# Weights read two bytes late, the first gates as a second product, and a planner that lets TensorE wait

## The chip, the cores and the metric

The kernel runs on one core of a Trainium2 chip (trn2). The metric is the device time of one execution in microseconds (us); lower is better.

## What is computed

```python
def _attn_ref(q, k, v, s):                  # 4 batches, 8 heads, 576 tokens, 64 wide
    scores = scale * np.matmul(q, k.transpose(0, 1, 3, 2))
    cum = np.cumsum(np.maximum(s, 0.0), axis=-1)
    bias = -(cum[:, :, :, None] - cum[:, :, None, :])
    scores = np.where(causal, -1000000000.0, scores + np.minimum(bias, 0.0))
    ...                                     # softmax over keys
    return np.matmul(attn, v)
def _moe_ref(x, w_gate, w_val, w_out, rms_g):   # 2304 tokens, 512 -> 1536 -> 512
    xn = x / np.sqrt(np.mean(x * x, axis=-1, keepdims=True) + 1e-06) * rms_g
    g = xn @ w_gate
    return g * (1.0 / (1.0 + np.exp(-g))) * (xn @ w_val) @ w_out
```

`reference` puts the heads of a token side by side, sends the result through `_moe_ref` and that result through a second block of the same kind without the normalisation (`_moe2_ref`, its own weights). The weights arrive as 8-byte floats; q, k, v and s as 4-byte floats.

## The kernel before

**Stages.** The 576 queries of a batch are cut in a group A (the first 256) and a group B (the other 320). The kernel starts with the A groups of batches 0 and 1: 16 "early" heads (`EarlyUnit`) with plain fp32 products. Then come group B of batches 0 and 1 and both groups of batches 2 and 3 (`Unit`), with split operands. Between them, on TensorE, run the gate and value products of the first MoE block (`moe1`) for each group of tokens whose heads are done and normalised (`normalise`). What `moe1` makes goes to DRAM (`h_d`), and after the attention is through, the out product of block 1 (`out_mm`) and block 2 follow.

**Split weights.** Every MoE product is exact enough only with more than one pass: a matrix is kept as H, its value rounded to TensorE's fp32r, and L, the rest, and one product is xH·H + xL·H + xH·L. `convert` makes H and L from the 8-byte words, 128 x 512 words at a time: a load into a tile `raw` (L382, 512 KB); ACT turns the top 16 bits into an fp16 (L384) and moves 16 bits of the lower half (L386), both into a tile `cvy`; DVE shifts and masks the upper words in `raw` (L389) and joins them with `cvy` by and/or (L392); a copy on ACT or POOL rounds to H (L396, L397); a subtraction gives L (L400). `load_gv` does this for the 12 slices f of gate and value weights of a block, two blocks each. For the first MoE block the raw words of slice f lie in the places of H and L of slice f+2 (`raw_places`).

**Order of the work.** Nothing is issued where it is written. Each call of `op` records one operation with a price per engine, what it reads and writes, and a priority. `Plan.run` then plays the program: per engine a heap `waiting` (by the time at which the inputs are there) and a heap `ready` (by priority); of what is ready on an engine, the lowest priority number goes first, and the order found is the order in which each engine's instructions are issued. `LAT` has the latencies between engines. Early head u has the priority P_ATT + u, the loads 1000 less, the MoE products of the first block P_MOE + f, which is higher than any head's: they fill in.

**The bias of the early heads.** `setup` (from L430) loads s, makes its running sum on DVE in `cum` (L473 to L481, the scan at L476), stores it (L484), and on POOL builds the identity (the affine select of `masks.py`), clears rows 64 and up of the early q and k tiles `lq` and sets row 64 of the q side to one (`clear_rows`, L458 and L459; its output is called "lower rows"). Row 64 of the k side gets the head's running sum by a DMA of 1 KB (L705), which waits for both. So one product over 128 rows (L716) gives scores and key bias at once. `self.least` takes minimum and mask on DVE, `exponent` is an ACT pass (L612), `values` transposes on TensorE (L726), copies to `pTA` (L732), multiplies with v (L736).

**Normalisation.** `normalise` squares x on ACT, sums squares by a product with `half` (L767), runs some 18 tiny steps on DVE (L795 to L829), transposes (L833), copies, spreads the factors by a product with `sel` (L840), scales x on DVE (L844) and splits it into xH (ACT, L847) and xL (L849). Then `gate_value` (L860) can read it, and `hidden` (L867 to L872) does tanh and the two multiplications.

## Time and profile before

| | |
|---|---|
| median of 3 runs (1147.38 to 1148.27) | 1148.12 us |
| the profiled execution / its span | 1150.81 us / 1148.8 us |
| granted TensorE clock, mean | 0.994 |
| busy: TensorE, its weight loads, DVE, ACT, POOL | 1119.8, 1002.3, 608.5, 545.9, 188.8 us |
| chain of waits: TensorE, DMA, DVE, ACT | 89%, 3%, 3%, 2% |
| moved by DMA | 112.54 MB, 98 GB/s on average |

The time of the profiled execution is the device time of that one run; the span is what the profile covers of it, from the first instruction to the last. Busy is time in which an engine works on an instruction. The chain of waits is followed back from the last instruction, at each step to what released it.

### The profile page before, as it was taken

What the parts mean: (1) busy time and instruction counts of PE and PEld (TensorE: products, weight loads), DVE (VectorE), ACT (ScalarE), POOL (GpSimd) and SP (SyncE); (2) the same over time, 40 slices, a digit from 0 to 9 for tenths busy, and PEclk for the clock granted to TensorE, in tenths of its full rate; (3) what the DMA queues carried; (4) which work ended last, traced back from release to release, by engine and by line L of the source; (5) the groups of instructions that cost most, each with busy time, mean ns of one, the idle gap of its engine ahead of it and who ended that gap; (6) DMA issues with size and microseconds to landing.
All of it is one profiled execution on the core that took longest, in us unless ns stands there. A gap on an engine that the chain in (4) does not pass through costs nothing.

```text
span 1148.8 us, 18822 instructions
## 1 busy us (share of the span) xinstructions
PE 1119.8 (97%) x6708; PEld 1002.3 (87%) x6708; DVE 608.5 (53%) x1670; ACT 545.9 (48%) x1203; POOL 188.8 (16%) x280
## 2 busy tenths in 40 slices
PE   5899999999999999999999999999999999999998
PEld 3589999999999999999877788888888888888898
DVE  5798899988735965542586424432222222222222
ACT  5787989888534844431687435432111211211121
POOL 3243445344202400000011000001000100000000
PEclk9899999999999999999999999999999999999999
DMA  5774455434221234438656634211000100100010
GB/s 156 229 239 130 141 146 155 123 102 128 75 74 46 71 102 116 113 109 273 224 165 201 203 110 130 74 37 49 26 1 1 64 1 1 46 1 1 1 37 20
DMA packets 70221, 112.54 MB, mean 98 GB/s; under 512 B 11696, under 2 KB 39344, under 8 KB 70128
## 3 DMA queue, kind: packets, MB, share of 16 engines
q1 hardware_dynamic: 70128, 111.35, 31.6%
q8 instruction: 53, 0.87, 0.3%
q14 instruction: 40, 0.33, 0.1%
HBM read 87.63 MB, written 23.67 MB: 97 GB/s over the span
## 4 chain that ended last, share of the span: by engine, by line
PE 89%; DMA 3%; DVE 3%; ACT 2%; issue 1%; SPq 1%; POOL 0%; DVEq 0%; ACTq 0%
PE mo L860 51%; PE sps L1013 8%; PE tp L1013 8%; PE mo L1013 5%; PE sps L575 4%; PE tp L639 4%; PE tp L655 4%; DMA cvs<-in_w_gv 1%; PE mo L767 1%; PE tp L736 1%; PE sps L716 1%; DMA raw<-in_w_gv 1%; ACT cvy L384 1%; DMA lq<-cum 1%; ACT cvy L386 1%
## 5 line engine op out<-in xcount | busy, mean ns | idle before, releaser
L860 PE MATMUL mo<-xH,L 128*128 128x320 f32 (+1 forms) x768 | 229.4, 299 | 0.0
L860 PE MATMUL mo<-xH,H 128*128 128x320 f32 (+1 forms) x768 | 229.0, 298 | 0.1
L860 PE MATMUL mo<-xL,H 128*128 128x320 f32 (+1 forms) x768 | 228.3, 298 | 0.5 <-POOL xL L849 0.5
L869 DVE SCALAR_TENSOR_TENSOR t<-t,mo 128x256 f32<-128x256 f32 (+2 forms) x156 | 81.3, 521 | 257.6 <-ACT t L867 257.1
L867 ACT ACTIVATE t<-mo 128x256 f32<-128x256 f32 (+2 forms) x156 | 72.3, 464 | 276.8 <-PE mo L860 271.9
L860 PE MATMUL mo<-x1H,L 128*128 128x512 f32 (+1 forms) x480 | 176.6, 368 | 0.0
L860 PE MATMUL mo<-x1H,H 128*128 128x512 f32 (+1 forms) x480 | 176.6, 368 | 0.0
L860 PE MATMUL mo<-x1L,H 128*128 128x512 f32 (+1 forms) x480 | 176.6, 368 | 0.0
L1002 ACT ACTIVATE hH<-hh 128x512 fp32r<-128x512 f32 (+1 forms) x120 | 69.6, 584 | 165.1 <-DVE hh L872 132.2
L860 PEld LDWEIGHTS mo<-xL,H 128*128 128x128 f32 x768 | 145.1, 189 | 1.4 <-POOL xL L849 0.7
L860 PEld LDWEIGHTS mo<-xH,H 128*128 128x128 f32 x768 | 145.0, 189 | 1.1 <-issue 0.3
L860 PEld LDWEIGHTS mo<-xH,L 128*128 128x128 f32 x768 | 145.0, 189 | 0.5
L872 DVE TENSOR_TENSOR hh<-t,mo 128x256 f32<-128x256 f32 (+2 forms) x156 | 81.3, 521 | 100.2 <-PE mo L860 99.2
L1004 DVE TENSOR_TENSOR hL<-hh,hH 128x512 fp32r<-128x512 f32 (+1 forms) x120 | 79.7, 667 | 87.7 <-ACT hH L1002 87.2
L860 PEld LDWEIGHTS mo<-x1H,L 128*128 128x128 f32 x480 | 90.5, 189 | 14.9
L860 PEld LDWEIGHTS mo<-x1H,H 128*128 128x128 f32 x480 | 90.5, 189 | 14.8
L860 PEld LDWEIGHTS mo<-x1L,H 128*128 128x128 f32 x480 | 90.5, 189 | 14.8
L612 ACT ACTIVATE sc<-sc,col 128x512 f32<-128x512 f32 (+4 forms) x160 | 95.6, 598 | 14.1 <-DVE col L601 13.2
L1045 POOL TENSOR_TENSOR x1L<-x1l,x1H 128x512 fp32r<-128x512 f32 (+1 forms) x20 | 25.8, 1302 | 390.6 <-ACT x1H L1043 302.4
L1013 PE MATMUL sps<-hH,oH 128*128 128x512 f32 (+1 forms) x192 | 67.8, 365 | 2.1 <-ACT hH L1002 2.1
L1013 PE MATMUL sps<-hL,oH 128*128 128x512 f32 (+1 forms) x192 | 69.5, 363 | 0.0
L1013 PE MATMUL tp<-hH,oL 128*128 128x512 f32 (+1 forms) x192 | 69.4, 363 | 0.0
(127 smaller groups left out, 2096.1 us busy)
## 6 DMA issues: line engine op xcount, KB each, us to landing
raw<-in_w_gv SPq DMA_DIRECT2D x40, 512.0 KB, 4.8
cvs<-in_w_o SPq DMA_DIRECT2D x24, 512.0 KB, 3.8
hh<-h_d SPq DMA_DIRECT2D x48, 256.0 KB, 3.1
cb<-cum_d SPq DMA_DIRECT2D x32, 288.0 KB, 3.4
lq<-in_qk SPq DMA_DIRECT2D x32, 288.0 KB, 3.2
h_d<-hh SPq DMA_DIRECT2D x72, 128.0 KB, 2.2
vl<-in_vp SPq DMA_DIRECT2D x32, 160.0 KB, 3.0
cvs<-in_w_gv SPq DMA_DIRECT2D x8, 512.0 KB, 4.2
```

Source lines behind the costliest of these rows:

```text
L575: op(PE, c_mm(n), lambda en, pt=pt, o=o, c=c, n=n, z=z, kk=kk: en.matmul(pt()[:, :n], qst[j]()[:, o:o + 128], kk()[:, c:c + n], start=z == ...
L612: op(ACT, c_act(o + m, 2) + 35, lambda en: en.activation(sc()[:m, :o + m], sc()[:m, :o + m], ACTF.Exp, scale=-1.0, bias=col()[:m, 0, t:t + 1],
L639: op(PE, C_TR, lambda en, pt=pt, a=a, m=m, kb=kb, t=t: en.transpose(pt()[:, a:a + P], self.sc[t]()[:, kb * P:kb * P + P], ident()), r=[sel ...
L655: op(PE, c_mm(n), lambda en, w=w, z=z, kb=kb, d0=d0, n=n, o=o, kn=kn: en.matmul(po()[:, o:o + n], vst[j]()[:kn, kb, :], pT[g][z]()[:kn, d0 ...
L860: op(PE, c_mm(n), lambda en, a=a, x=x, c=c, k=k, i=i: en.matmul(ps()[:, :n], a()[:, c], x()[:, k, :n], start=(k == 0 and i == 0), stop=(k ...
L867: op(ACT, c_act(n), lambda en: en.activation(t()[:, :n], gp()[:, :n], ACTF.Tanh, scale=0.5), r=[gp], w=[t], pri=pri)
L869: op(DVE, c_tt(n), lambda en: en.scalar_tensor_tensor(out=t()[:, :n], in0=t()[:, :n], scalar=1.0, in1=gp()[:, :n], op0=ALU.add, op1=ALU.mu ...
L872: op(DVE, c_tt(n), lambda en: en.tensor_tensor(out=hh()[:, :n], in0=t()[:, :n], in1=vp_()[:, :n], op=ALU.mult), r=[vp_, t], w=[hh], pri=pri)
L1002: op(ACT, c_act(n) + 35, lambda en: en.activation(H()[:, :n], hh()[:, :n], ACTF.Copy), r=[hh], w=[H], pri=pri)
L1004: op(DVE, c_tt(n), lambda en: en.tensor_tensor(out=L()[:, :n], in0=hh()[:, :n], in1=f32(H()[:, :n]), op=ALU.subtract), r=[hh, H], w=[L], p ...
L1013: op(PE, c_mm(n), lambda en, d=d, c=c, w=w, x=x, i=i: en.matmul(acc_[d]()[:, :n], Wo[w]()[:, c], HL[x]()[:, :n], start=(f == 0 and i == 0) ...
L1045: op(POOL, c_ptt(n), lambda en, k=k, x=x: en.tensor_tensor(out=L()[:, k, :n], in0=x()[:, :n], in1=f32(H()[:, k, :n]), op=ALU.subtract), r= ...
```

## The change

**Weights.** The load reads the same words from two bytes on (2047 of 2048 16-bit units per partition), so that what was in bytes 2 to 5 of each word is now a whole 32-bit unit. One ACT pass still puts the fp16 of the top bits in the upper half of `cvy`, whose lower half is zeroed once (`clear`). One DVE instruction shifts the 32-bit unit right by 13 and ors `cvy` in, and writes the result into the raw tile. The ACT pass of L386 and the DVE pass of L389 are gone; H and L read the raw tile, which is therefore held until L is done. `cvy` is two tiles of their own for the first weights, one for all later ones.

**First gates.** The running sum is made twice: for the first 256 tokens into `cumA`, and later for all. The first four early heads get no row of the sum; a second product (L761 of the changed kernel) of a column of the identity, broadcast, with `cumA` adds it to their scores. The other twelve load the row from `cumA`.

**Planner.** An operation of TensorE whose last input came from another engine enters the `ready` heap 1500 ns (`SLACK`) later than its inputs are there; until then it is in `at_once`, from which it is taken only where `ready` holds nothing. The raw loads have other priorities, conversions too, and the sums of squares another price.

```diff
+    SLACK = 1500.0
...
         def offer(n):
             for k, (e, _) in enumerate(ops[n][0]):
-                heapq.heappush(waiting[e], (ready_on[n][k], k, n))
+                slack = 0.0
+                if e == PE and released[n] not in (PE, NONE):
+                    heapq.heappush(at_once, (ready_on[n][k], k, n))
+                    slack = self.SLACK
+                heapq.heappush(waiting[e], (ready_on[n][k] + slack, k, n))
...
+                if e == PE and not ready[e]:
...
+                    if at_once and (not waiting[e] or at_once[0][0] < waiting[e][0][0]):
+                        t, k, n = at_once[0]
+                        if t <= free[e]:
+                            heapq.heappop(at_once)
+                            heapq.heappush(ready[e], (ops[n][3] + 1.0e6 * k, n))
...
+                    if ready_on[u][k] > before:
+                        released[u] = e
...
+FIRST = 4
...
-        op(SP, 8 * P * n, lambda en: en.dma_start(out=stage(), in_=src.bitcast(I32)),
+        op(SP, 8 * P * n, lambda en: en.dma_start(
+            out=stage().bitcast(U16)[:, :4 * n - 1], in_=src.bitcast(U16)[:, 1:]),
            w=[stage], pri=pri if early is None else early)
         op(ACT, c_act(n) + 165, lambda en: en.activation(
-            part(y, F16, 2, 1), part(stage, BF16, 4, 3), ACTF.Copy), r=[stage], w=[y], pri=pri)
-        op(ACT, c_act(n) + 165, lambda en: en.activation(
-            part(y, U16, 2, 0), part(stage, U16, 4, 1), ACTF.Copy, scale=2.0 ** -13,
-            bias=-4095.5 * 2.0 ** -13), r=[stage], w=[y], pri=pri)
-        op(DVE, c_ts(n), lambda en: en.tensor_scalar(
-            out=hi(), in0=hi(), scalar1=3, scalar2=MIDDLE,
-            op0=ALU.logical_shift_left, op1=ALU.bitwise_and), r=[stage], w=[stage], pri=pri, port=True)
+            part(y, F16, 2, 1), part(stage, BF16, 4, 2), ACTF.Copy), r=[stage], w=[y], pri=pri)
         op(DVE, c_tt(n), lambda en: en.scalar_tensor_tensor(
-            out=i32(y), in0=i32(y), scalar=-(1 << 27) + 7, in1=hi(),
-            op0=ALU.bitwise_and, op1=ALU.bitwise_or), r=[stage, y], w=[y], pri=pri, port=True)
+            out=whole(U32), in0=whole(U32), scalar=13, in1=y().bitcast(U32),
+            op0=ALU.logical_shift_right, op1=ALU.bitwise_or), r=[stage, y], w=[stage],
+           pri=pri, port=True)
...
+        def clear_cum(en):
+            en.memset(cumA()[NB * NH:64], 0.0)
+            en.memset(cumA()[64:], 0.0)
+        op(POOL, 500, clear_cum, w=[(cumA, 1)], pri=-2e6)
...
+        cumulate(cumA, 2 * P, -1e6)
+        cumulate(cum, S, -900)
...
-            op(SP, 1024, lambda en: en.dma_start(
-                out=ql()[D:D + 1, 1, 288 * i:288 * i + 256], in_=cum()[n:n + 1, 0:256]),
-               r=[cum, "lower rows"], w=self.parts[2:], pri=pri)
+            if not self.first:
+                op(SP, 1024, lambda en: en.dma_start(
+                    out=ql()[D:D + 1, 1, 288 * i:288 * i + 256], in_=cumA()[n:n + 1]),
+                   r=[cumA, "lower rows"], w=self.parts[2:], pri=pri)
...
-                    start=True, stop=True), r=[*self.parts, "lower rows"], w=[pt], pri=pri)
+                    start=True, stop=not self.first), r=[*self.parts, "lower rows"], w=[pt],
+                   pri=pri)
+                if self.first:
+                    i = self.b * NH + self.h
+                    op(PE, 0.422 * 4 * kl, lambda en, pt=pt, kl=kl: en.matmul(
+                        pt()[:, :kl], ident()[:, i:i + 1].to_broadcast([P, P]), cumA()[:, :kl],
+                        start=False, stop=True), r=[ident, cumA], w=[pt], pri=pri)
...
-            op(PE, 108 * nt, sums, r=[q, half], w=[ps], pri=pri)
+            op(PE, 206 * nt, sums, r=[q, half], w=[ps], pri=pri)
...
-        W1.append(load_gv(w_gv, f, places, tmps1, P_ATT + 10 + 0.5 * f,
-                          P_ATT - 1000 + 6 + 1.5 * f))
+        W1.append(load_gv(w_gv, f, places, tmps1, P_ATT + 8 + 0.5 * f,
+                          P_ATT - 1000 + 8 + 1.0 * f))
```

The order on three stretches follows; a row is a line of the kernel, the operation, out<-in by tile names and the shape, and a number behind a tile's name tells its uses apart.

TensorE, its first rows, before; `sps` is a bank for scores, `tp` one for transposes, `sc` a tile of scores:

```order
L716 MATMUL sps_165<-lq_101 128x128
L716 MATMUL sps_168<-lq_101 128x256
L716 MATMUL sps_177<-lq_106 128x128
L726 MATMUL tp_181<-ident,sc_170 128x128
L716 MATMUL sps_185<-lq_106 128x256
L726 MATMUL tp_181<-ident,sc_179 128x128 x2
L716 MATMUL sps_201<-lq_101 128x128
```

TensorE, its first rows in the change:

```order
L755 MATMUL sps_151<-lq_116 128x128
L755 MATMUL sps_164<-lq_116 128x256
L761 MATMUL sps_164<-cumA,ident 128x256
L761 MATMUL sps_151<-cumA,ident 128x128
L755 MATMUL sps_180<-lq_121 128x128
L761 MATMUL sps_180<-cumA,ident 128x128
L755 MATMUL sps_186<-lq_121 128x256
L761 MATMUL sps_186<-cumA,ident 128x256
L771 MATMUL tp_193<-ident,sc_171 128x128
```

Each of the first scores is now followed by a product with `cumA`, and both products of the second head come ahead of the first transposes.

ACT, its first rows, before; `tot` takes the row sums, `col` the row's decay:

```order
L384 ACT_TABLE_LOAD
L384 ACTIVATE cvy<-raw_154 128x512
L386 ACTIVATE cvy<-raw_154 128x512
L612 ACTIVATE sc_170,tot_89<-sc_170,col_171 128x128
L612 ACTIVATE sc_179,tot_89<-sc_179,col_171 128x256
L396 ACTIVATE H_190<-cvy 128x512
L612 ACTIVATE sc_187,tot_89<-sc_187,col_188 128x128
L384 ACTIVATE cvy<-raw_161 128x512
L612 ACTIVATE sc_195,tot_89<-sc_195,col_188 128x256
```

ACT, its first rows in the change:

```order
L649 ACT_TABLE_LOAD
L649 ACTIVATE sc_171,tot_89<-sc_171,col_172 128x128
L649 ACTIVATE sc_177,tot_89<-sc_177,col_172 128x256
L649 ACTIVATE sc_188,tot_89<-sc_188,col_189 128x128
L408 ACTIVATE cvy<-raw_166 128x512
L649 ACTIVATE sc_196,tot_89<-sc_196,col_189 128x256
L649 ACTIVATE sc_210,tot_89<-sc_210,col_211 128x128
L415 ACTIVATE H_222<-raw_166 128x512
```

The first pass over the weights moved from the first place on ACT to behind three passes of the softmax, and of the two conversion passes per `raw` tile one is left.

TensorE, around the transposes (L833) of the first normalisation of a B group, before; `xH`, `xL`, `L`, `H` belong to gate and value products, `qst`, `kHH`, `kLL` to scores of later heads:

```order
L833 MATMUL mo_2642<-ident,sq_87 128x128 x3
L639 MATMUL tp_2635<-ident,sc_2519 128x128
L639 MATMUL tp_2635<-ident,sc_2527 128x128
L860 MATMUL mo_2605<-xH_1288,L_1080 128x256
L860 MATMUL mo_2605<-xH_1288,H_1057 128x256
L860 MATMUL mo_2605<-xL_1267,H_1057 128x256
L860 MATMUL mo_2605<-xH_1288,L_1080 128x256
L639 MATMUL tp_2671<-ident,sc_115 128x128
L639 MATMUL tp_2671<-ident,sc_2519 128x128
```

TensorE, around the last gate or value product (L905) of the two early groups in the change; the next such product stands 48 rows later, behind the normalisation of the first B group:

```order
L612 MATMUL sps_2443<-kHH_848,qst_97 128x288
L612 MATMUL sps_2443<-kLL_879,qst_97 128x288
L905 MATMUL mo_2389<-xH_1351,L_1222 128x256
L612 MATMUL sps_2451<-kHH_848,qst_97 128x288
L612 MATMUL sps_2451<-kLL_879,qst_97 128x288
L676 MATMUL tp_2456<-ident,sc_111 128x128
L676 MATMUL tp_2456<-ident,sc_2227 128x128
L676 MATMUL tp_2456<-ident,sc_2236 128x128
L676 MATMUL tp_2456<-ident,sc_111 128x128
L676 MATMUL tp_2456<-ident,sc_2227 128x128
L612 MATMUL sps_2466<-kHH_984,qst_99 128x384
L612 MATMUL sps_2466<-kLL_1025,qst_99 128x384
```

Before, gate and value products of the early groups still stood behind the transposes of that normalisation; in the change they are used up ahead of it.

## Rows read from the trace of the kernel before

**Rows 1.** Page, part 1: busy us (share of the span) and instructions of TensorE.
```profile
PE 1119.8 (97%) x6708; PEld 1002.3 (87%) x6708; DVE 608.5 (53%) x1670; ACT 545.9 (48%) x1203; POOL 188.8 (16%) x280
```

**Rows 2.** Windows: busy us (x instructions) of PE, PEld, DVE, ACT, POOL; PEclk, DMA share, GB/s.
```profile
0.00:12.00 12.00, 0.41 (x2) 0.45 (x3) 4.66 (x15) 0.81 (x1) 6.41 (x21) 1.00 0.48 134
12.00:42.00 30.00, 26.23 (x137) 17.80 (x136) 22.15 (x81) 26.01 (x73) 8.19 (x9) 1.00 0.69 199
42.00:56.00 14.00, 11.74 (x43) 7.54 (x42) 11.27 (x42) 11.22 (x29) 3.80 (x5) 0.63 0.83 245
56.00:80.00 24.00, 21.28 (x156) 18.98 (x156) 21.66 (x52) 21.04 (x49) 10.80 (x13) 1.00 0.73 214
80.00:300.00 220.00, 218.04 (x1655) 210.53 (x1654) 196.46 (x735) 185.60 (x468) 100.39 (x164) 1.00 0.45 134
...
560.00:650.00 90.00, 87.24 (x378) 69.96 (x377) 63.17 (x100) 67.63 (x117) 11.78 (x8) 1.00 0.56 180
...
1144.00:1148.80 4.80, 0.93 (x8) 0.72 (x7) 1.19 (x3) 0.38 (x1) 0.00 (x0) 0.94 0.33 111
```

**Rows 3.** Waits of PE, whole run: waiting line, what ended it, us in total, times, longest.
```profile
PE sps L716 <- DMA lq<-cum: 13.4, 2, 11.6
```

**Rows 4.** Timeline, first 20 us, all engines: start us, us, engine line operation.
```profile
3.80 0.51 POOL L458 MEMSET lq<- 1x256 f32 x1
4.09 1.35 DVE L476 TENSOR_TENSOR_SCAN cum<-cum 32x576 f32<-32x576 f32 x1
...
5.74 0.39 POOL masks.py:199 TENSOR_SCALAR_AFFINE_SELECT ident<-ident 128x128 f32<-128x128 f32 x1
...
7.60 2.49 SPq L705 DMA_DIRECT2D lq<-cum  x4
...
11.59 2.08 PE L716 MATMUL sps<-lq 128*128 128x128 f32 x6 [11.59 <-DMA lq<-cum]
```

**Rows 5.** Timeline, PE alone, 14 to 29 us: the early score products.
```profile
14.61 1.06 PE L716 MATMUL sps<-lq 128*128 128x256 f32 x2
...
19.02 0.82 PE L716 MATMUL sps<-lq 128*128 128x128 f32 x4
...
28.07 0.60 PE L716 MATMUL sps<-lq 128*128 128x256 f32 x2
```

**Rows 6.** Tile raw, whole run: forms with min/median/max ns, and landing times of its loads.
```profile
L386 ACT ACTIVATE cvy<-raw x40: 751/774/802, 13.1 to 615.6; 128x512 uint16<-128x512 uint16 x40
L389 DVE TENSOR_SCALAR raw<-raw x40: 414/423/1196, 13.3 to 616.4; 128x512 int32<-128x512 int32 x40
L392 DVE SCALAR_TENSOR_TENSOR cvy<-cvy,raw x40: 678/693/1595, 14.0 to 616.9; 128x512 int32<-128x512 int32 x40
...
DMA to landing us min/median/max: 3.7/4.8/7.0
```

**Rows 7.** Timeline, PE, 38 to 49 us: the stalls of heads 11 and 12.
```profile
41.25 0.89 PE L716 MATMUL sps<-lq 128*128 128x128 f32 x4 [1.82 <-DMA lq<-cum]
...
48.62 0.33 PE L726 MATMUL tp<-ident,sc 128*128 128x128 f32 x1 [1.50 <-ACT sc L612]
```

**Rows 8.** Timeline, PE, 159 to 185 us: normalisation of the first B group.
```profile
159.96 0.83 PE L767 MATMUL mo<-half,sq 128*128 128x2 f32 x6
...
182.92 0.49 PE L833 MATMUL mo<-ident,sq 128*128 128x128 f32 x3
...
184.11 0.41 PE L840 MATMUL mo<-xL,sel 128*128 128x320 f32 x1
```

**Rows 9.** Groups of instructions on DVE, 100 to 300 us: count, busy us, mean ns, idle before.
```profile
L647 DVE TENSOR_TENSOR pTB<-tp,pTB 128x512 fp32r<-128x512 f32 (+1 forms) x74 | 42.0, 571 | 5.7 <-ACT pTB L644 4.9
L601 DVE CUSTOM_DVE_ANT_0 sc<-sps,cb 128x384 f32<-128x384 f32 (+3 forms) x85 | 37.3, 448 | 2.6 <-PE sps L575 1.8 <-PE tp L639 0.2
...
L813 DVE SCALAR_TENSOR_TENSOR rc<-rc 128x3 f32<-128x3 f32 (+1 forms) x9 | 1.5, 166 | 0.1
```

**Rows 10.** Timeline, ACT, 185 to 186 us: the first normalised copy.
```profile
185.78 0.47 ACT L847 ACTIVATE xH<-x 128x320 fp32r<-128x320 f32 x1 [0.24 <-DVE x L844]
```

More of the change, by code (lines that the diff above doesn't have):

```diff
@@ L397, in convert @@
-            POOL: lambda en: en.tensor_scalar(out=H()[:, cut], in0=y(), scalar1=1.0, scalar2=1.0,
-                                              op0=ALU.mult, op1=ALU.mult)},
-           r=[y], w=[(H, c)], pri=pri)
+            ACT: lambda en: en.activation(H()[:, cut], whole(), ACTF.Copy),
+            POOL: lambda en: en.tensor_scalar(out=H()[:, cut], in0=whole(), scalar1=1.0,
+                                              scalar2=1.0, op0=ALU.mult, op1=ALU.mult)},
+           r=[stage], w=[(H, c)], pri=pri)
@@ L400, in convert, with clear @@
         op(sub, 0, lambda en: en.tensor_tensor(
-            out=L()[:, cut], in0=y(), in1=f32(H()[:, cut]), op=ALU.subtract),
-           r=[y, (H, c)], w=[(L, c)], pri=pri, port=True)
+            out=L()[:, cut], in0=whole(), in1=f32(H()[:, cut]), op=ALU.subtract),
+           r=[stage, (H, c)], w=[(L, c)], pri=pri, port=True)
+    def clear(tiles, pri):
+        for b in tiles:
+            op([(POOL, 500), (DVE, 320)], 0, lambda en, b=b: en.memset(b(), 0.0), w=[b], pri=pri)
     def raw_places(last):
@@ L472, in setup, with cumulate, steps @@
         op([(POOL, 1500), (DVE, 1500)], 0, clear_scores, w=sc4, pri=-1e5)
-        op(DVE, 400, lambda en: en.tensor_scalar(
-            out=cum(), in0=cum(), scalar1=0.0, scalar2=None, op0=ALU.max),
-           r=[cum], w=[cum], pri=-1e6)
-        op(DVE, 670, lambda en: en.tensor_tensor_scan(
-            cum2(), cum(), cum(), 0.0, op0=ALU.add, op1=ALU.max),
-           r=[cum], w=[cum2], pri=-1e6)
-        op(DVE, 400, lambda en: en.tensor_scalar(
-            out=cum(), in0=cum2(), scalar1=cum2()[:, S // 2:S // 2 + 1], scalar2=1.0 / SCALE,
-            op0=ALU.subtract, op1=ALU.mult), r=[cum2], w=[cum], pri=-1e6)
+        def cumulate(out, n, pri):
+            rows = NB * NH
+            def steps(en):
+                en.tensor_scalar(out=cum()[:, :n], in0=cum()[:, :n], scalar1=0.0, scalar2=None,
+                                 op0=ALU.max)
+                en.tensor_tensor_scan(cum2()[:, :n], cum()[:, :n], cum()[:, :n], 0.0,
+                                      op0=ALU.add, op1=ALU.max)
+                en.tensor_scalar(out=out()[:rows, :n], in0=cum2()[:, :n],
+                                 scalar1=cum2()[:, n // 2:n // 2 + 1],
+                                 scalar2=1.0 / SCALE, op0=ALU.subtract, op1=ALU.mult)
+            op(DVE, 400 + 3.6 * n, steps, r=[cum], w=[cum, cum2, (out, 0)] if out is not cum
+               else [cum, cum2], pri=pri)
+        cumulate(cumA, 2 * P, -1e6)
+        cumulate(cum, S, -900)
         op(SP, 4 * NB * NH * S, lambda en: en.dma_start(out=cum_d, in_=cum()),
-           r=[cum], w=["cum_d"], pri=-1e6)
+           r=[cum], w=["cum_d"], pri=-990)
     def lq_parts(b, half):
@@ L687, in __init__ @@
             self.parts = lq_parts(early_q[i % 2], i // 2 % 2)
+            self.first = i < FIRST
             self.vl = early_v[i % 2], i // 2 % 2
@@ L900, in tile_kernel @@
     places = raw_places([buf("at", f"pTB{i}", [P, 1024], I32, f"cvs{i}") for i in range(2)])
+    tops1 = [buf("at", f"cvt{i}", [P, 512], F32, "cvy") for i in range(2)]
     cvt = [0]
@@ L904, in tmps1 @@
         cvt[0] += 1
[L905 removed]
+        return tops1[cvt[0] % 2]
+    clear(tops1, P_ATT + 2)
     heads, units = [], []
```

25 lines of the change are left out of this document (13 added, 12 removed).

## The prediction

> **What bounds the kernel now.** I read five views: the page's busy shares, a table of windows, TensorE's waits, the timeline of the first 50 us, and the stretch around one normalisation.
>
> The page has TensorE busy for 1119.8 us of a span of 1148.8 [rows 1]; only its 29.0 idle us, and work added to it or taken from it, can move the time. The windows say where they are [rows 2]: 11.59 of the first 12 us, 3.77 in 12 to 42, 2.26 in 42 to 56, 2.72 in 56 to 80, 1.96 in 80 to 300, 2.76 in 560 to 650, 3.87 at the end, hardly any elsewhere. The reader is also to see two other things in those rows: the granted clock is 0.63 in 42 to 56, where DMA is at its busiest (245 GB/s, share 0.83), and ACT is busy for 26.01 of the 30 us from 12 to 42, so that there ACT nearly bounds too.
>
> The waits name the first hole: 13.4 us for the DMA that puts the running sum into `lq`, 11.6 of them once [rows 3]. The timeline has the steps [rows 4]: POOL clears the last rows at 4.31, the scan ends at 5.44, the identity is there at 6.13, the four small DMAs are issued from 7.60, and the first score product starts at 11.59.
>
> **The start: −6.** The first products no longer need the running sum, only q, k and the cleared rows. Two more memsets stand ahead of the clearing; at 0.3 to 0.5 each as for the rows of that line [rows 4] the first product starts at about 5.2, and its gate product when the identity is there, 6.13 + 0.6 to 0.8, near 7. The sum of 256 columns takes less than half the scan's 1.35 and is no longer last. TensorE gains 11.59 − 5.5 = 6 us. Bounds: 8 (if nothing but the clearing holds it) and 3 (if the gate products hold up the two score banks, so that only two heads' products gain).
>
> **Eight gate products: +3.2.** A head's score products, 128 and 256 columns, take 0.82 [rows 5], and a gate product has the same columns and type: 4 × 0.82 = 3.3, less a little for overlap. The rows give bounds: 128x256 twice took 1.06 at 14.61 and 0.60 at 28.07 [rows 5], though the clock column says 1.00 for both [rows 2]. If all the eight are at the early pace it is 4.6, if at the later one 2.6. The Trainium skill ("TensorE: Matmul & The Clock Gate", part 1) says that the engine's default is throttled and that activity releases it; by that the early pace holds at the start and the term is 4.6. I stay with 3.2, since the 0.82 are of the same stretch.
>
> **The conversions: −3.5.** An ACT pass of 0.774 and a DVE pass of 0.423 fall away per block [rows 6]. The first weights have 24 blocks, all before about 110 us: 24 × 0.774 = 18.6 us of ACT and 24 × 0.423 = 10.2 of DVE, the other 48 blocks lie later. TensorE had 3.77 + 2.26 + 2.72 = 8.75 us idle from 12 to 80 [rows 2]; 1.82 ended with the running sum's DMA [rows 7], and 0.7 I put down to other transfers. Of the remaining 6.2, which end mostly with ACT or DVE (such as 1.50 for a softmax pass [rows 7]), I take a good half, 3.5. Bounds: 0 (the load, not the pass, is what conversion waits for) and 6.2. The remaining DVE instruction reads and writes every other word, as the old one read one of its inputs; I keep its 0.693 [rows 6].
>
> **The shifted load: 0.** It moves two bytes less per partition. No row of before has such a load; a raw load lands after 3.7 to 7.0, median 4.8 [rows 6]. The near row is the unshifted one, so I take no difference; the far end, landings beyond 7 us, is the second rival. The Trainium skill ("DMA: Bandwidth & Descriptors", "How a descriptor splits into AXI transactions") has it that a read starts at the 256-byte line below its address: bytes 2 to 4095 touch the same sixteen lines as 0 to 4095, so by it nothing changes either way if each partition's read is one descriptor.
>
> **The stretch at half clock: 0.** 14 us at 0.63 [rows 2] are worth about 14 × 0.63 = 8.8 of full clock: some 5 us more could be had back or lost again. Whether it recurs hangs on holes in TensorE's work around 40 to 56; load and softmax stay what they were, so I take it as it is. Bounds −4.5 and +4.5.
>
> **The late stalls: −2.5.** At 560 to 650 and 80 to 300 TensorE idles 2.76 + 1.96 = 4.7 us [rows 2]. With the new rule a product that another engine has just released stands behind others that are ready, which puts 1.5 us of work between; and ACT and DVE have fewer passes there (48 blocks × 0.774 and 0.423, [rows 6]). I take half. Bounds 0 and −4.7.
>
> **The order around the first B group: +5.** This is what the order rows show against the change. Before, gate products of the early groups still stood behind the transposes (L833) of the normalisation of the first B group; now they are used up 32 rows ahead of it, and 47 rows pass without one. Before, the chain from the last sum of squares to the transposes took from 160 to 182.92 [rows 8], and nobody felt it. Now what TensorE has between the squares and the transposes is about 9 us by the rows of order: two heads' value products, 16 gate products, transposes and scores. DVE has in the same piece the 18 tiny steps at about 0.17 to 0.2 (3.4), 11 copies and subtractions and 11 minimum passes at 0.45 to 0.57 [rows 9], two groups' tanh products: some 12 us. So about 3.5 are open. From the transposes to the first xH it took 182.92 to 186.25 [rows 8, 10], 3.3, against some 2 of scores and transposes: 1.5 more. Sum 5. Bounds 0 (the heap at priority lets DVE do the steps first) and 9 (a second B group does the same).
>
> **The sum.** −6 + 3.2 − 3.5 + 0 + 0 − 2.5 + 5 = −3.8, on the profiled execution's 1150.81 about 1147.0. The median of before is 1148.12, 2.7 lower; on its scale that is 1144.3, and I say **1144.0**. A measurement of this kernel tells about 0.2%, 2.3 us, from no change: faster is below 1145.8, slower above 1150.4.
>
> **The rivals.**
>
> 1. *Better: the run-out is covered and the half-clock stretch is gone.* For it: ACT loses a pass of 0.774 per block in just the stretch where it is fullest. Then +5 falls away and 4.5 come on top: 1134.5. Against it: DMA is as busy as before there. Chance 0.22.
>
> 2. *Slower: shifted words land late.* If a load that starts at an odd pair of bytes takes half again its 4.8 us, 24 loads of 512 KB (12.6 MB, at 245 GB/s 51 us of the first 80) no longer fit beside the heads' own, and gate products wait. By 24 × 0.5 us, 12 more: about 1155. It decides from landings above some 7 us [rows 6]. No row excludes it. Chance 0.08.
>
> 3. *Slower: the run-out is wholly exposed.* If the 23 us from squares to transposes [rows 8] remain, the 9 us of other products leave 14 open instead of 3.5: 1144 + 9 to 10, near 1153.5. It decides once that chain is longer than some 18 us. Against it: it was so long because nothing hurried it: 18 steps of 0.17 are 3 us of work [rows 9]. Chance 0.12.
>
> 4. *No change: the start's gain is swallowed.* The first heads start 6 us earlier, but the loads of words and later heads end when they did, since the stretch from 42 to 56 is at 245 GB/s [rows 2]. Then TensorE waits there instead, −6 falls to about −2: 1148. Here belongs also that the planner's rule does nothing that the chip shows, so that the late stalls stay (−2.5 goes): 1146.5. Chance 0.15.
>
> **How the numbers follow.** Forecast 0.43, rivals 0.22, 0.08, 0.12, 0.15. The forecast's own range, by its larger bounds (the conversions ±3, the run-out −5 to +4, the half clock ±4.5), is 1139 to 1149. The range with 8 in 10 reaches down to the first rival and up to the fourth and the milder end of the third: 1133 to 1152; above it lie the second and most of the third, below it little. Faster: most of the forecast (0.34), all of the first, a little of the fourth, 0.58; slower: the second, the third and an edge of the forecast, 0.21; within 0.2% the rest, 0.21.
>
> **What would show it right or wrong.** Right: first score product near 5.2 to 5.5 and a gate product near 7; no wait for `lq<-cum` of over 2 us; the passes of L386 and L389 gone, raw landings near 4.8; TensorE busy for about 1123 us; a hole of some us ahead of the first gate products of the first B group, somewhere in 155 to 180; hardly a wait at 560 to 650. Wrong: raw landings above 7; a hole at 40 to 56 larger than the 2.26 of before; a clock below 0.9 in a stretch other than that one; the remaining DVE pass much over 0.69, which would give back what the dropped one saves.

## The result, and the profile after

The changed kernel takes 1137.38 us (median, 1136.85 to 1139.23) against 1148.19 for the kernel before: a ratio of 0.9908, 95% interval 0.9893 to 0.9922, so 10.8 us faster. One of the four runs of the kernel before took 1460.04 us; the ratio leaves it out, and the median of the other three is the 1148.12 of the table further up. The prediction was 1144.0 in a range of 1133 to 1152: right in its direction and inside the range, but 6.6 us too high. The profiled execution has 1137.85 us and a span of 1136.0, against 1150.81 and 1148.8: 12.8 us of span are to be found. The profiled run of the kernel before was 2.7 us above its median, that of the changed kernel 0.5, so about 2 of the 12.8 us belong to these single runs and not to the change.

Part 1 of the page of the changed kernel, to be held against [rows 1]:

```profile
PE 1115.4 (98%) x6724; PEld 1002.4 (88%) x6724; DVE 583.3 (51%) x1607; ACT 512.5 (45%) x1129; POOL 185.8 (16%) x281
```

The span less TensorE's busy time is 20.6 us, where it was 29.0. So 8.4 us come from idle time. The other 4.4 come from TensorE's busy time itself, although eight products were added to it.

1.7 us of that busy time are a stretch at half clock which the trace of the kernel before has and that of the changed kernel has not (window of the kernel before):

```profile
420.00:426.00 6.00, 6.00 (x40) 5.96 (x39) 3.54 (x12) 2.48 (x5) 1.03 (x1) 0.72 0.31 65
```

A granted clock of 0.72 over 6 us is 6 × 0.28 = 1.7 us of full clock (2.4 GHz) lost to the lower level (1.2 GHz). TensorE was busy all the time there, with gate products behind sums of squares of two columns each. In the changed kernel the same window has 1.00. The mean granted clock of that profiled run is 0.994; the median of 50 other runs of the kernel before is 0.997.

The windows of the changed kernel, with the columns of [rows 2]:

```profile
0.00:12.00 12.00, 6.31 (x18) 4.68 (x19) 8.11 (x26) 3.35 (x8) 7.79 (x24) 1.00 0.59 163
12.00:42.00 30.00, 27.54 (x156) 18.98 (x154) 23.04 (x81) 23.14 (x67) 8.41 (x8) 1.00 0.72 211
42.00:56.00 14.00, 11.12 (x43) 8.22 (x43) 10.09 (x33) 10.48 (x27) 4.68 (x6) 0.63 0.84 285
56.00:80.00 24.00, 24.00 (x192) 22.92 (x192) 21.11 (x62) 16.17 (x38) 12.98 (x13) 1.00 0.58 182
80.00:300.00 220.00, 216.55 (x1642) 211.29 (x1641) 168.11 (x611) 160.74 (x398) 88.12 (x145) 1.00 0.43 124
...
560.00:650.00 90.00, 90.00 (x397) 73.97 (x396) 41.10 (x60) 48.78 (x80) 10.93 (x8) 1.00 0.64 202
```

Idle of TensorE, before and after: 11.59 and 5.69 in the first 12 us, 8.75 and 5.34 from 12 to 80, 1.96 and 3.45 from 80 to 300, 2.76 and none from 560 to 650; the rest went from 3.9 to 6.1, most of it from 650 to 1100 (none before, 1.5 after, waits for ACT's `oo`). The windows are fixed in time, so the later ones hold work that stood some 9 us later before. The stretch from 42 to 56 has its 0.63 again.

TensorE's timeline of the changed kernel, rows of the first 17 us (start, length, line, operation):

```profile
4.67 1.62 PE L755 MATMUL sps<-lq 128*128 128x128 f32 x4 [4.67 <-DMA lq<-in_qk]
6.38 1.65 PE L761 MATMUL sps<-cumA,ident 128*128 128x256 f32 x4
...
10.82 1.06 PE L761 MATMUL sps<-cumA,ident 128*128 128x256 f32 x2
...
16.62 0.59 PE L761 MATMUL sps<-cumA,ident 128*128 128x256 f32 x2
```

The first product starts at 4.67 instead of 11.59 and its gate product at 6.38. Two gate products of 256 columns take 1.06 early on and 0.59 at 16.62, just as the score products of [rows 5] did.

The tile `raw` in the changed kernel, to be held against [rows 6]:

```profile
L408 ACT ACTIVATE cvy<-raw x40: 759/782/802, 11.4 to 577.4; 128x512 f16<-128x512 bf16 x40
L410 DVE SCALAR_TENSOR_TENSOR raw<-raw,cvy x40: 678/693/1797, 13.7 to 578.3; 128x512 uint32<-128x512 uint32 x40
...
DMA to landing us min/median/max: 3.6/5.0/7.3
```

Two passes per block are left of four, the DVE one at 0.693 as before; landing has a median of 5.0 where it was 4.8.

TensorE in the changed kernel around the run-out of early gate products, from the last sum of squares (L812) over the transposes (L878) to the first gate products of the first B group:

```profile
165.66 0.72 PE L812 MATMUL mo<-half,sq 128*128 128x2 f32 x6
...
171.01 0.28 PE L905 MATMUL mo<-xH,L 128*128 128x256 f32 x1
...
171.89 0.76 PE L676 MATMUL tp<-ident,sc 128*128 128x128 f32 x5 [0.33 <-DVE x L701]
...
173.20 0.44 PE L676 MATMUL tp<-ident,sc 128*128 128x128 f32 x2 [0.19 <-DVE pTB L684]
174.08 0.47 PE L612 MATMUL sps<-kHH,qst 128*128 128x512 f32 x1 [0.45 <-DVE col L638]
...
177.15 0.55 PE L878 MATMUL mo<-ident,sq 128*128 128x128 f32 x3
...
178.56 0.84 PE L885 MATMUL mo<-xL,sel 128*128 128x320 f32 x4
...
180.58 1.22 PE L905 MATMUL mo<-xH,H 128*128 128x320 f32 x4 [0.30 <-ACT xH L892]
```

From 171.01 to 180.58 no gate or value product runs, as the order said. TensorE idles for 0.33 + 0.19 + 0.45 + 0.30 = 1.3 us in it.

The start of the last gate or value product of the first block divides each trace in two. Timeline of TensorE, before:

```profile
548.61 0.31 PE L860 MATMUL mo<-xH,L 128*128 128x320 f32 x1
```

and in the changed kernel:

```profile
539.84 0.31 PE L905 MATMUL mo<-xH,L 128*128 128x320 f32 x1
```

So 8.8 us are gained up to here, and 600.2 − 596.2 = 4.0 us between here and the end of the span. But the line doesn't cut the work alike: 3 of the 1440 products of the two out stages stand ahead of it before and 11 in the changed kernel, at about 0.2 us each. From the start of the 21st out product (552.66 and 542.07) to the end of the span it is 596.1 and 593.9, so 2.2 us are gained behind and 10.6 ahead, with the 1.7 us at half clock among them.

### The profile page after: what moved, and what is told of

Same layout as the page of the kernel before. It is cut to its first block, busy times and chain, and to the rows that moved or that the text cites. A ratio compares the mean times of both kernels' runs of the same rounds, so it can differ in the third digit from the quotient of the medians.

```text
span 1136.0 us, 18676 instructions
## 1 busy us (share of the span) xinstructions
PE 1115.4 (98%) x6724; PEld 1002.4 (88%) x6724; DVE 583.3 (51%) x1607; ACT 512.5 (45%) x1129; POOL 185.8 (16%) x281
## 4 chain that ended last, share of the span: by engine, by line
PE 88%; DVE 2%; ACT 1%; issue 0%; DMA 0%; POOL 0%; DVEq 0%; SPq 0%; ACTq 0%
PE mo L905 50%; PE tp L1061 10%; PE sps L1061 10%; PE mo L1061 6%; PE tp L692 4%; PE tp L676 4%; PE sps L612 4%; PE mo L812 1%; DVE sc L638 1%; DVE pTB L684 0%; DMA x_d<-oo 0%; PE mo L885 0%; DVE x L889 0%; ACT pTB L681 0%; PE mo L878 0%
## 5 line engine op out<-in xcount | busy, mean ns | idle before, releaser
L905 PE MATMUL mo<-xH,H 128*128 128x320 f32 (+1 forms) x768 | 228.4, 299 | 0.3 <-ACT xH L892 0.3
L905 PE MATMUL mo<-xL,H 128*128 128x320 f32 (+1 forms) x768 | 228.1, 297 | 0.1
L905 PE MATMUL mo<-xH,L 128*128 128x320 f32 (+1 forms) x768 | 227.0, 296 | 0.0
L905 PE MATMUL mo<-x1L,H 128*128 128x512 f32 (+1 forms) x480 | 176.6, 368 | 0.0
L905 PE MATMUL mo<-x1H,H 128*128 128x512 f32 (+1 forms) x480 | 176.6, 368 | 0.0
L905 PE MATMUL mo<-x1H,L 128*128 128x512 f32 (+1 forms) x480 | 176.6, 368 | 0.0
L905 PEld LDWEIGHTS mo<-xH,H 128*128 128x128 f32 x768 | 144.4, 188 | 1.8 <-ACT xH L892 0.7
L905 PEld LDWEIGHTS mo<-xL,H 128*128 128x128 f32 x768 | 144.4, 188 | 0.9 <-POOL xL L894 0.3
L905 PEld LDWEIGHTS mo<-xH,L 128*128 128x128 f32 x768 | 144.2, 188 | 0.6 <-issue 0.2
L905 PEld LDWEIGHTS mo<-x1H,H 128*128 128x128 f32 x480 | 90.5, 189 | 14.9
L905 PEld LDWEIGHTS mo<-x1H,L 128*128 128x128 f32 x480 | 90.5, 189 | 14.8
L905 PEld LDWEIGHTS mo<-x1L,H 128*128 128x128 f32 x480 | 90.5, 189 | 14.8
L1061 PE MATMUL tp<-hH,oH 128*128 128x512 f32 (+1 forms) x192 | 69.7, 364 | 1.5 <-ACT oo L1070 1.5
L1061 PE MATMUL tp<-hL,oH 128*128 128x512 f32 (+1 forms) x192 | 69.7, 363 | 0.0
```

The lines of the kernel that those rows point to most:

```text
L905: op(PE, c_mm(n), lambda en, a=a, x=x, c=c, k=k, i=i: en.matmul(ps()[:, :n], a()[:, c], x()[:, k, :n], start=(k == 0 and i == 0), stop=(k ...
L1061: op(PE, c_mm(n), lambda en, d=d, c=c, w=w, x=x, i=i: en.matmul(acc_[d]()[:, :n], Wo[w]()[:, c], HL[x]()[:, :n], start=(f == 0 and i == 0) ...
```

## The experiments

Twelve kernels ran, each timed in five rounds beside the kernel before. "Up to" is the start of the last gate or value product of block 1, "rest" the span less that, "from 21st" the span less the start of the 21st out product (or of that last gate or value product, if it comes later); "gap" is the longest time between two gate or value products from 100 to 400 us, with TensorE's idle time in it. "Clock" is the mean granted clock of the profiled run. Each kernel has one trace, and the three groups of kernels were timed on different chips, where the median of the kernel before was 1148.03, 1147.84 and 1147.14.

| kernel | median us | ratio, 95% interval | up to | rest | from 21st | gap (idle) | clock |
|---|---|---|---|---|---|---|---|
| before | 1148.19 | 1 | 548.6 | 600.2 | 596.1 | 3.2 (0) | 0.994 |
| changed | 1137.38 | 0.9893 to 0.9922 | 539.8 | 596.2 | 593.9 | 9.6 (1.3) | 0.995 |
| no_slack | 1141.28 | 0.9924 to 0.9959 | 541.8 | 596.4 | 595.0 | 4.3 (0) | 0.999 |
| no_gate | 1138.17 | 0.9895 to 0.9927 | 539.3 | 596.5 | 594.2 | 5.4 (0.6) | 0.995 |
| old_words | 1147.91 | 0.9986 to 1.0008 | 543.9 | 601.9 | 600.4 | 20.5 (1.6) | 0.995 |
| old_prio | 1138.48 | 0.9904 to 0.9946 | 539.0 | 597.7 | 596.9 | 31.4 (2.9) | 1.000 |
| before_words | 1143.15 | 0.9944 to 0.9974 | 542.9 | 598.2 | 594.5 | 3.8 (0) | 0.999 |
| before_slack | 1158.01 | 1.0069 to 1.0100 | 555.1 | 600.8 | 597.4 | 27.7 (3.8) | 0.996 |
| only_gates | 1145.79 | 0.9964 to 0.9989 | 543.8 | 601.5 | 597.5 | 3.9 (0) | 0.998 |
| early_old | 1141.24 | 0.9925 to 0.9953 | 542.1 | 598.3 | 596.1 | 20.5 (1.6) | 0.998 |
| add_act | 1136.43 | 0.9885 to 0.9920 | 537.4 | 596.2 | 595.3 | 6.7 (0.2) | 0.997 |
| add_dve | 1145.58 | 0.9968 to 0.9989 | 544.7 | 599.8 | 597.7 | 20.7 (1.6) | 0.993 |
| slack_800 | 1143.07 | 0.9948 to 0.9975 | 544.4 | 596.8 | 593.1 | 4.0 (0.6) | 0.997 |
| slack_2500 | 1168.08 | 1.0173 to 1.0202 | 564.5 | 601.0 | 601.0 | 36.3 (6.7) | 0.988 |

**Undoing one part of the changed kernel.** `no_slack`:

```diff
-    SLACK = 1500.0
+    SLACK = 0.0
```

> The changed kernel with SLACK = 0, so that the planner orders as it did before; words and first gates stay. Theory 1 (the parts add up, each in its place): the late stalls of the before kernel come back (2.8 us at 560 to 650) and so do the longer slots of products behind small waits (about 5 us less in the changed kernel); the first 12 us stay as in the change: about 1144 to 1146. Theory 2 (the planner's rule is the whole gain and the rest cancels): 1147 to 1149. Theory 3 (any new order moves the time by some us, the rule itself does nothing): within 3 us of 1137.

1141.28, 3.9 slower, between theories 1 and 3. But where theory 1 expected the stalls from 560 to 650 back, they stayed away but for 0.4 us: they are not mainly the planner's doing.

`no_gate`:

```diff
-FIRST = 4
+FIRST = 0
```

> The changed kernel with FIRST = 0: all sixteen early heads get the row of the running sum by DMA, now from the short sum; no gate products. Theory 1: the first product waits again for the sum's row, at about 10 to 10.5 (short sum done about 5.8, row issued with the loads, some 2 us to land and issues ahead of it), 4 to 5 us of the start are lost, 4.7 us of gate products saved, so the time changes by less than 1.5 us: 1136 to 1139. Theory 2 (the early heads are bound by loads and ACT anyway, so an early start is swallowed): 4.7 us of products gone and nothing lost: 1133. Rival: the later start delays all that follows and TensorE's early work is not the bound: +5: 1142.

1138.17, as theory 1 had it, though the first product starts sooner than the 10 us expected. It waits for the row of the sum (timeline of TensorE):

```profile
8.70 2.08 PE L755 MATMUL sps<-lq 128*128 128x128 f32 x6 [8.70 <-DMA lq<-cumA]
```

That is 4.0 us later than in the changed kernel, and the 4.7 us of gate products are gone. The gate products themselves gain nothing that can be told. The short sum and its place alone bring the first product from 11.59 to 8.70, 2.9 us.

`old_words` (the conversion of before, with its unshifted load and its tiles for `cvy`; the two passes that come back are shown):

```diff
...
+        op(ACT, c_act(n) + 165, lambda en: en.activation(
+            part(y, U16, 2, 0), part(stage, U16, 4, 1), ACTF.Copy, scale=2.0 ** -13,
+            bias=-4095.5 * 2.0 ** -13), r=[stage], w=[y], pri=pri)
+        op(DVE, c_ts(n), lambda en: en.tensor_scalar(
+            out=hi(), in0=hi(), scalar1=3, scalar2=MIDDLE,
+            op0=ALU.logical_shift_left, op1=ALU.bitwise_and), r=[stage], w=[stage], pri=pri, port=True)
...
```

> The changed kernel with the conversion of before: unshifted loads, two ACT and two DVE passes per block, cvy in the tiles of before; planner and first gates stay. Theory 1: the idle time from 12 to 80 us rises again by some 3 us, the late part little: 1140 to 1142. Theory 2 (planner alone): within 1 us of 1137. Rival: shifted loads are slower (landing 5.0 against 4.8 us in the profiles) and cost what the passes save: 1135 to 1137.

1147.91: the whole gain is gone, 10.5 us, beyond every expectation. 4.1 of the profile's 9.8 us lie ahead of the last gate product and 5.7 behind. They don't lie where theory 1 looked for them: TensorE idles for 5.4 us from 12 to 80, as in the changed kernel (5.3). Waits of TensorE from 560 to 700 us (what waits, on what, total, times, longest), in old_words:

```profile
PE mo L1064 <- ACT hH L1053: 2.5, 3, 1.1
PE sps L1064 <- ACT hH L1053: 0.9, 2, 0.7
PE tp L1064 <- ACT hH L1053: 0.6, 1, 0.6
PE sps L1064 <- DVE hL L1055: 0.5, 1, 0.5
```

and in the changed kernel:

```profile
PE tp L1061 <- ACT oo L1070: 1.0, 1, 1.0
```

The waits for the split of `hh` (hH, hL) are back, 4.5 us where there is 1.0 for something else. Behind the last gate or value product such waits come to 2.8 to 4.5 us in the four kernels with the old late words, and to 0 to 1.9 in the seven with the new ones and a rule of 0 to 1500 ns that have no pass added.

`old_prio` (raw loads at 6 + 1.5 f, conversions at 10 + 0.5 f, 108 for the sums):

> The changed kernel with the raw loads' and conversions' priorities and the price of the sums of squares as before. Theory 1 (no term in the prediction): within 1.5 us of 1137. Rival: the priorities carry part of the gain in the stretch from 12 to 80: 1140. If it moves by more than 2 us with no place where it shows, the order's own scatter is of that size (theory 3).

1138.48, within 1.5 us. Its gap is 31.4 us with 2.9 us of idle time in it, so even a long run-out is mostly filled (timeline of TensorE: the last early gate product, the last sum of squares of the first B group, its transposes):

```profile
156.04 0.28 PE L905 MATMUL mo<-xH,L 128*128 128x256 f32 x1
...
162.30 0.83 PE L812 MATMUL mo<-half,sq 128*128 128x2 f32 x6
...
183.96 0.50 PE L878 MATMUL mo<-ident,sq 128*128 128x128 f32 x3
```

Its granted clock from 42 to 56 is 1.00 where the changed kernel has 0.63, and it is no faster.

**One part alone on the kernel before.** `before_words` has the new conversion and nothing else of the change:

> The kernel before with the shifted words alone (one ACT and one DVE pass per block fewer, its own cvy tiles); planner, sum of the gates and priorities as before. Undoing the words in the changed kernel cost 10.5 us. Theory 1 (the words are the larger part wherever they stand: the early conversions and the late ones are both on TensorE's way): 1139 to 1142, with no waits of TensorE at 560 to 650. Theory 2 (the words only bring much where the planner's rule and the early start make ACT and DVE the bound): 1144 to 1147.

1143.15, between the theories: 5 us, half of what undoing the words cost. The waits at 560 to 650 go to 0.05 us of idle time. Part of the 5 us goes with the clock: the runs at a mean granted clock of 0.999 took 1142.93 (median of three), and the kernel before at 0.999 or 1.0 took 1146.48 (median of 11 of the 50 runs made beside the experiments), 3.5 more; at 0.994 or 0.995 it took 1149.53 (median of five).

`before_slack` has the new planner and nothing else:

> The kernel before with the planner's rule alone (SLACK 1500). Undoing it in the changed kernel cost 3.9 us. Theory 1 (additive): 1144 to 1145. Theory 2 (the rule needs ACT and DVE with room: a product that is set back later frees its bank later): 1147 to 1150, no gain.

1158.01: 10 us slower, more than the second theory gave. TensorE's timeline there, rows of the sums of squares (L790), the transposes (L856), of the gate products that frame the gap (L883) and of the waits between:

```profile
163.63 0.73 PE L790 MATMUL mo<-half,sq 128*128 128x2 f32 x6
...
170.79 0.28 PE L883 MATMUL mo<-xH,L 128*128 128x256 f32 x1
...
173.25 1.51 PE L678 MATMUL tp<-pTB,vst 128*128 128x320 f32 x10 [0.79 <-DVE pTB L670]
...
176.58 0.77 PE L662 MATMUL tp<-ident,sc 128*128 128x128 f32 x5 [0.47 <-DVE x L687]
...
177.80 0.73 PE L790 MATMUL mo<-half,sq 128*128 128x2 f32 x6
...
184.58 0.47 PE L598 MATMUL sps<-kHH,qst 128*128 128x512 f32 x1 [0.53 <-DVE rc L833]
185.56 1.51 PE L678 MATMUL tp<-pTB,vst 128*128 128x320 f32 x10 [0.28 <-DVE pTB L670]
...
188.97 1.23 PE L662 MATMUL tp<-ident,sc 128*128 128x128 f32 x7 [0.78 <-DVE x L687]
...
191.25 0.47 PE L598 MATMUL sps<-kHH,qst 128*128 128x512 f32 x1 [0.50 <-DVE col L624]
...
194.32 0.72 PE L790 MATMUL mo<-half,sq 128*128 128x2 f32 x6
...
195.26 0.49 PE L856 MATMUL mo<-ident,sq 128*128 128x128 f32 x3
...
197.97 0.41 PE L863 MATMUL mo<-xL,sel 128*128 128x320 f32 x1 [0.47 <-DVE x L867]
198.52 0.79 PE L883 MATMUL mo<-xH,H 128*128 128x320 f32 x2
199.98 0.42 PE L883 MATMUL mo<-xL,H 128*128 128x320 f32 x1 [0.67 <-POOL xL L872]
```

From 170.79 to 198.52 no gate product runs. The group has four sums of squares, one for each pair of heads. The last two come at 163.63 and 177.80, 14 us apart, and the one at 194.32 is the first of the next group, 17 us later: the heads alone don't go fast, and TensorE waits on DVE again and again, 3.8 us in the gap. From 80 to 300 it idles for 7.9 us, where it was 2.0 before; the rest of the 10 us isn't traced. Right behind it the granted clock falls, windows of the same run:

```profile
195.00:200.00 5.00, 3.73 (x22) 2.62 (x21) 4.86 (x11) 4.64 (x11) 3.86 (x7) 1.00 0.54 151
200.00:205.00 5.00, 5.00 (x26) 5.00 (x27) 1.38 (x8) 1.83 (x5) 1.83 (x2) 0.66 0.32 87
205.00:210.00 5.00, 5.00 (x39) 4.91 (x38) 3.91 (x12) 4.05 (x11) 1.65 (x4) 1.00 0.12 33
```

0.66 in 200 to 205 is a stretch in part at the lower of the two levels, 1.2 GHz, after 1.27 us idle in the five before. In the changed kernel the early gate products are used up at the same time, 171.01; but there the last sum of squares had come at 165.66, 12 us earlier, and the transposes followed 11.5 us behind it, not 17.5. That the heads are further on when the other products run out doesn't decide the cost alone: in old_prio those products end at 156.04, 6 us ahead of the group's last sum (162.30), and the kernel is as fast as the changed one.

`only_gates` (SLACK 0, old words, old priorities in the changed kernel):

> The kernel before with the first gates alone (two sums, cumA, eight gate products, table load first); SLACK 0, old words, old priorities. First product at about 4.7 instead of 11.6. Theory 1: 6.9 us earlier, 4.7 us of added products, so within 3 us of before: 1145 to 1148. Theory 2 (the early start is swallowed by ACT, DVE and loads of the early heads): 4 us slower or no gain: 1148 to 1152. Theory 3 (the whole start counts): 1142 to 1143.

1145.79, theory 1: of the 6.9 us that the first product starts earlier, 2 are left once the 4.7 us of gate products are paid.

**Early or late words.** `early_old` has the old conversion where `early is not None`, so for the 24 blocks of the first weights only:

> The changed kernel with the old conversion for the 24 blocks of the first weights only (raw landing in the first 110 us); the later 48 blocks stay new. Theory 1 (half the words' 10.5 us comes early, half late): 1142 to 1143. Theory 2 (it is the late stretch at 560 to 650, where TensorE's waits of 2.8 and the out products' longer slots of 3.2 came back with the old words): 1138 to 1140. Theory 3 (it is the early stretch alone): 1147.

1141.24, on the edge between theories 1 and 2. By these single kernels 3.9 us belong to the early blocks and 6.7 to the late ones; differences of this size are within the scatter told below.

**Which pass.** `add_act` doubles the ACT pass over the top bits, `add_dve` adds a DVE pass that changes nothing:

```diff
...
+        op(ACT, c_act(n) + 165, lambda en: en.activation(
+            part(y, F16, 2, 1), part(stage, BF16, 4, 2), ACTF.Copy), r=[stage], w=[y], pri=pri)
...
```

```diff
...
+        op(DVE, c_ts(n), lambda en: en.tensor_scalar(
+            out=whole(I32), in0=whole(I32), scalar1=0, scalar2=-1,
+            op0=ALU.logical_shift_left, op1=ALU.bitwise_and), r=[stage], w=[stage], pri=pri, port=True)
...
```

> The changed kernel with its ACT pass over the top bits done twice per block: one ACT pass of 0.78 us more for each of the 72 blocks, as many as before had, no DVE pass more. Undoing the words cost 10.5 us (of which 6.7 in the 48 late blocks). Theory ACT (what the words give is the ACT pass, since the late waits end with ACT's split of hh): 1143 to 1146. Theory DVE (it is the DVE pass): 1138 to 1139. Theory chain (the length of a block's chain, so both passes by their time, 0.78 to 0.42): 1143 to 1144 here and 1140 to 1141 with the DVE pass.

> The changed kernel with one DVE pass more per block in place on the raw tile (a shift by nothing and a mask of ones, 128x512 words, about 0.42 us), no ACT pass more. Theory ACT: 1138 to 1139. Theory DVE: 1143 to 1146. Theory chain: 1140 to 1141.

Part 1 of the page of add_act:

```profile
PE 1114.4 (98%) x6724; PEld 1001.4 (88%) x6724; DVE 589.0 (52%) x1606; ACT 556.2 (49%) x1197; POOL 191.5 (17%) x286
```

and of add_dve:

```profile
PE 1119.4 (98%) x6724; PEld 1002.8 (88%) x6724; DVE 608.6 (53%) x1662; ACT 514.5 (45%) x1139; POOL 195.2 (17%) x288
```

ACT works 43.7 us more (556.2 against 512.5; some of the work that the planner may put on several engines went to DVE and POOL) and the time is 1136.43, not slower at all. DVE works 25.3 us more and the time is 1145.58, 8.2 slower, 4.9 of the span ahead of the last gate product and 3.6 behind it. The clock doesn't make this difference: at a mean granted clock of 0.993 to 0.995 the runs of add_dve took 1145.38 to 1146.16 and those of the changed kernel, at 0.994 and 0.995, 1136.90 to 1139.23. Theory ACT and theory chain fall: the doubled ACT pass lengthens every block's chain by more than the DVE pass does. But the late waits for the split of `hh` are not what costs the time. They come back with the ACT pass, without loss (waits of TensorE from 560 to 700 us in add_act):

```profile
PE sps L1063 <- ACT hH L1052: 1.2, 2, 0.7
PE mo L1063 <- DVE hL L1054: 1.0, 1, 1.0
```

With the DVE pass they are 1.1 us. Where `cvy` lies differs between the old and the new words too, and no run tests that alone; add_dve, with the tiles of the change, lost 8.2 of the 10.5 us.

**The size of the rule.**

> The changed kernel with SLACK 800 in place of 1500 (0 gave 1141.3). If the rule works by its size: between, 1138 to 1140. If half of it is enough to bridge the small waits (each below 1 us) without using up the gate products early: 1135 to 1137, a better kernel than either. If the order's own scatter rules: anywhere in 1136 to 1144.

> The changed kernel with SLACK 2500. If the rule works by its size: 1135 to 1137. If a longer hold slows the heads and uses up the gate products of the early groups still earlier, as with the rule alone on the kernel before (1158.0): 1140 or more, with a hole on TensorE at 160 to 200.

0, 800, 1500 and 2500 ns give 1141.3, 1143.1, 1137.4 and 1168.1: no trend. 2500 has two gaps, of 28.4 and 36.3 us, and around the second the idle time is 7.2 us and the granted clock 0.95 (window):

```profile
300.00:400.00 100.00, 92.78 (x664) 87.38 (x664) 72.96 (x268) 62.06 (x161) 27.98 (x52) 0.95 0.27 83
```

800 is slower than none although its only change is the order. It is the measure of scatter: up to the last gate product the kernels with the new words, the short sum and a rule of 0 to 1500 ns lie between 537.4 and 544.4. A single difference of 1 to 4 us in that part (no_slack, no_gate, old_prio, the early share of the words) is therefore not a price of the part undone. The part behind scatters less, if it is counted alike. From the 21st out product on it is 596.1 to 600.4 in the four kernels with old late words and 593.1 to 596.9 in the seven with the new ones, 3.0 us apart in the mean, though the ranges touch; it is 597.7 with the DVE pass added and 595.3 with the ACT pass. slack_2500 (601.0) is left out. It comes there 25 us late, and its granted clock falls once more behind the line; so new words alone don't make this part short.

The medians tell the words more clearly. The five kernels with the dropped DVE pass, or one as long, in all blocks (before, old_words, before_slack, only_gates, add_dve) take 1145.6 to 1158.0; the eight others but slack_2500 take 1136.4 to 1143.2 (early_old, with it in a third of the blocks, 1141.2), and the one with the doubled ACT pass is the fastest of them. So it is shown that the words gain, and add_act and add_dve, one kernel each, put it down to DVE's pass. How many us the words are worth hangs on the order, 5 in one pair of kernels and 10.5 in another. None of these kernels is clearly faster than the changed one: add_act's interval covers its.

What the rule does shows inside TensorE's busy time. The gate and value products of block 1 are taken here from the start of each to the next start, idle time left out, and for those in stretches at half clock the time beyond the usual 0.118 us (256 columns) or 0.147 us (320 columns) too. They fill 312.0 to 314.6 us in the nine kernels with a rule of 1500 or 2500 ns, and 315.0 to 317.1 in the five with 0 or 800: 2.5 us apart in the mean, and no overlap. The time beyond the usual lies in the products that stand next to a product of another kind, 7.8 to 9.3 us in the nine and 11.3 to 13.3 in the five.

## Why the prediction was right, and where it missed

**The start, −6:** right, 11.59 − 5.69 = 5.9 us less idle. only_gates kept 2 of it, which is the start less the gate products (−6 + 4.7) and a little more; it is no sign of the fourth rival's swallowed start.

**Eight gate products, +3.2:** mis-sized. From the start of each to the next instruction they fill 4.7 us. Five of the eight ran at the early pace, 1.06 us for the 256 columns at 10.82, the other three at the later one, 0.59 at 16.62; the clock column shows 1.00 for both. All eight at the early pace would be 5.1 from start to start, 4 × (0.85 + 0.43), so that the bound of 4.6 was set too low and was met in part by luck. The Trainium skill ("TensorE: Matmul & The Clock Gate", part 1), on which the prediction drew for this bound, has the default state throttled; the trace agrees as far as the first products run at half the later pace.

**The conversions, −3.5:** the idle time from 12 to 80 fell by 3.4, from 8.75 to 5.34. But the reason isn't borne out by the runs, and the number may be luck. I counted on the 0.774 us ACT pass, since ACT was the busiest engine there; with an ACT pass of that length put in once more the stretch has 5.8 us idle, with the DVE pass 5.7. The words alone bring it to 5.7 (before_words), but the change without them does too, to 5.4 (old_words), where the gates or the rule alone leave it at 10.0 and 9.9. So it isn't shown what took the 3.4.

**The shifted load, 0:** right, a median of 5.0 to land against 4.8. The latest landing is 7.3, beyond the 7 of the prediction, but old_words, with unshifted loads, has 8.3: that is not the shift's. Medians are 4.8 to 5.2 in the four kernels with unshifted loads throughout. The trace agrees with what the prediction took from the Trainium skill ("DMA: Bandwidth & Descriptors", "How a descriptor splits into AXI transactions"). The second rival is out.

**The stretch at half clock, 0:** right in the profile, 0.63 again. Other kernels run it otherwise: the granted clock is 1.00 there in old_prio and before_words, and old_prio is no faster than the changed kernel (1138.48), so the first rival's 4.5 us for it are not seen.

**The late stalls, −2.5:** mis-sized and put down to the wrong part. 560 to 650 lost all of its 2.76, but 1.5 came up behind it, and from the 21st out product on 2.2 us are gained. I had named the planner's rule first; no_slack has 0.4 us of these stalls without it, and before_words loses them without it. It is the words that take the waits away. The half that I had taken off 80 to 300 went the other way, 1.96 to 3.45, mostly the 1.3 of the run-out.

**The run-out, +5:** this is the step that failed. The order was read rightly: the gap is there, at 171 to 181. It cost 1.3 us, not 5. I had set 9 us of other products against some 12 of DVE's work. From 165.66 to 177.15, 11.5 us, TensorE had 10.5 us of products, not 9, and DVE 10.7 us of work, not 12; so 1.0 was open instead of 3.5. From the transposes to the first gate product, 3.4 us, TensorE had 3.1 us of products, not 2, and 0.3 was open instead of 1.5. The products on TensorE were counted too low. The third rival was no phantom: with the rule alone (before_slack) the chain from the last sum to the transposes took 17.5 us, and the kernel was slower by 10, though only 3.8 us of that is idle time in the gap, not the 14 that the rival had. Length alone doesn't do it: in old_prio the chain took 21.7 us (162.30 to 183.96), past the rival's 18, for 2.9 us of idle time.

**Not in the sum:** TensorE's busy time fell by 4.4 with 4.7 added, so other products took 9.1 less. 1.7 of them are the stretch at half clock from 420 to 426 in the trace of the kernel before. From start to next start, idle left out, the gate and value products of block 1 went from 317.7 to 314.1 us, scores from 73.5 to 71.4, out products from 298.3 to 297.0, values from 61.9 to 60.6. Of the 3.6 us of the gate and value products 0.9 go with the half clock, and 2.7 are of the size of what goes with the planner's rule (above). The profile models the ends of pipelined products, so short waits may stand in a busy engine. What makes the rest is open, as is how much of the first part's gain is the order's luck.

So the span's sum, as measured: −5.9 (first 12 us) + 4.7 (gate products) − 3.4 (12 to 80) − 2.8 (560 to 650) + 1.5 (80 to 300, the run-out among it) − 9.1 (other products, 1.7 of them the half clock at 420 to 426) + 2.2 (idle elsewhere, 1.5 of it from 650 to 1100) = −12.8. Against the forecast's −3.8 that is 9.0 less: 3.7 by the run-out and 9.1 by the other products, against 1.5 more for the gate products and 2.2 of idle time elsewhere. 1137.38 lies below the forecast's own range of 1139 to 1149. It is inside the stated one because that was drawn down to the first rival, of which one half came true (the run-out was nearly covered) and the other did not (the half clock stayed).

## What to carry to other kernels

Where a planner sets the order, don't price a rule by undoing it once: the same rule was worth −4 in one kernel and +10 in another, and neighbouring values differ by 6 us without a trend. Compare stretches that scatter little, count the same work on both sides of a dividing line, hold the granted clocks of the runs side by side, and look for what is used up early. An engine that is busiest in a stretch need not be the one whose pass is worth removing; put the suspected pass in once more and see.
